# Re-emitting a long-convolution stage as a software pipeline over 128-channel units, with both forward transforms in shared matmuls

## The chip, the cores and the metric

The kernel runs on one core of one Trainium2 chip. Times are device microseconds (us) of one execution. The profile gives, for one execution, the busy time of each engine (PE is TensorE, PEld its weight loads, DVE is VectorE, ACT is ScalarE, SP is SyncE; a "q" behind a name, as in SPq, is the part of the engine that issues DMAs), what each instruction waited for, and the clock that TensorE was granted.

## The reference, cut to what matters

```python
# x, v, k: (1, 2048, 1024) bf16;  ssm_k: (1024, 2048)
a  = s5_ssm(x)                       # linear recurrence over time, complex state of 1024
kv = shift_conv(k, shift_k) * v      # 4-tap causal filter per channel, times v
y  = irfft(rfft(pad(kv)) * rfft(pad(ssm_k)))[:2048] + kv * ssm_D   # convolution of length 4096
b  = x * y
g  = sigmoid((x * gate_w).sum(-1))
out = g * a + (1 - g) * b
```

The change touches only `y`, which is called the convolution below. The convolution of 1024 channels is done with transforms written as matmuls.

## The kernel before

The program has four stretches: tables (to 35 us), the convolution, a change-over in which tables and scaled C matrices for the recurrence are made, and the scan part. The convolution works on four units of 256 channels. `front` makes the first stage of both forward transforms (`zk` from the filter, `zv` from `kv`), and each of 8 rounds does the second stages, the complex product, and the first inverse stage. `evict` means here the copy from PSUM (the matmul accumulator) to SBUF.

```python
def front(u):
    ka = load_K(u); zk = ...; stage1(ka, zk, 0)        # 8 x (4 matmuls, one eviction)
    for j in range(CH // 128):
        make_kv(u * (CH // 128) + j)                   # 4-tap filter; 3 tmpj multiplies on ScalarE; kv_scr <- acc
    va = load_A(kv_scr, u, "va")                       # same buffer as ka, bufs=1
    zv = ...; stage1(va, zv, 1)
    zs[u] = (zk, zv)

front(0)
for u in range(NU):                                    # NU = 4, CH = 256
    for kk in range(16 // KM):                         # 8 rounds
        ks = spectrum(zk, kk, fC, fS, fN, "ks")        # 6 matmuls, eviction on ScalarE
        vs = spectrum(zv, kk, fC, fS, fN, "vs")        # 6 matmuls, eviction on ScalarE
        ...                                            # t1, t2, pp: five products on VectorE
        qq = spectrum(None, kk, gC, gN, gS, "qq", inp=pp)   # 6 matmuls, eviction on ScalarE
        for i in range(KM):                            # 2 stores of 128 KB, one on SyncE, one on ScalarE
            (nc.sync if k2 % 2 == 0 else nc.scalar).dma_start(out=zb[k2:128:16, ...], in_=qq[:, i, ...])
    if u + 1 < NU: front(u + 1)
    for gg in ...:                                     # last stage: 4 matmuls, cv eviction on ScalarE, store
        nc.sync.dma_start(out=pB_scr..., in_=cv)
```

## Time and profile before

| | before |
|---|---|
| time | 761.41 us (761.37 to 761.45, 2 runs) |
| span of the profiled run | 758.3 us |
| last `cv` eviction (end of the convolution) | 426.6 us |
| from there to the end | 331.8 us |
| TensorE's granted clock, mean | 0.797 |

The page of the profile, kernel before: busy time by engine, then the span in 40 slices of 19 us (each digit is the busy share, or the clock, in tenths).

```profile
PE 449.9 (59%) x2013; PEld 218.6 (29%) x2048; DVE 431.5 (57%) x1022; ACT 368.7 (49%) x455; POOL 4.1 (1%) x10
...
PE   0030555438466546557564250679996997799567
...
DVE  6444657532323132222322513799999999998962
ACT  4765969437334543436333779722631552155022
...
PEclk9985667677767876767776665698998999899869
```

No engine stays full before slice 27. From there VectorE is at 9: the scan part is VectorE's. In the convolution (slices 3 to 23) ScalarE reaches 9 in two slices at the start, and then nothing stays above 6 for long, which is the mark of engines that wait for each other.

The groups table, kernel before: line, engine, operation, tiles, count | busy us, mean ns of one | idle time of the engine before them, and what ended it.

```profile
L333 PE MATMUL ps<-pp,gC 128*128 128x512 bf16 x64 | 36.4, 569 | 114.1 <-DVE pp L375 114.1
L318 PE MATMUL ps<-tab_188,ka 128*128 128x256 bf16 x256 | 44.5, 351 | 97.9 <-DMA ka<-kv_scr 52.0
L340 ACT CAST qq<-ps 128x1024 bf16<-128x1024 f32 x32 | 32.3, 1011 | 102.6 <-PE ps L338 102.6
```

TensorE waited 114.1 us for the product `pp`, and 52.0 us for `kv` to come back from memory. The timeline of one round shows the first wait:

```profile
207.11 0.42 DVE L375 TENSOR_TENSOR pp<-t_1036 128x512 bf16<-128x512 bf16 x1
207.59 0.61 PE L333 MATMUL ps<-pp,gC 128*128 128x512 bf16 x1 [3.43 <-DVE pp L375]
...
209.51 1.01 ACT L340 CAST qq<-ps 128x1024 bf16<-128x1024 f32 x1 [4.05 <-PE ps L338]
...
211.26 1.01 ACT L340 CAST ks<-ps 128x1024 bf16<-128x1024 f32 x1 [0.73 <-PE ps L338]
...
212.93 1.01 ACT L340 CAST vs<-ps 128x1024 bf16<-128x1024 f32 x1 [0.66 <-PE ps L338]
213.97 0.69 DVE L371 TENSOR_TENSOR t_1072<-ks,vs 128x1024 bf16<-128x1024 bf16 x1 [6.44 <-ACT vs L340]
```

The round is a loop: product, inverse matmuls, the forward matmuls of the next round, which stand behind the inverse ones in TensorE's queue, the `vs` eviction, and the product again. The longest wait of TensorE in it is 3.43 us, of ScalarE 4.05, of VectorE 6.44. The table of windows (busy us of each engine with its count, then the clock, the share of the DMA engines, GB/s) gives the sum for the convolution:

```profile
core 0: us, PE busy (x) PEld busy (x) DVE busy (x) ACT busy (x) POOL busy (x), PEclk, DMA share, GB/s
40.00:426.00 386.00, 202.89 (x884) 112.45 (x896) 137.15 (x237) 197.43 (x180) 0.00 (x0) 0.72 0.36 82
```

### The profile page before, as it was taken

To read this page: it belongs to the slowest core of one execution; us is meant where nothing else is said; L and a number is where in the kernel's file an instruction comes from. 1 tells how busy PE (TensorE), PEld (TensorE's weight loads), DVE (VectorE), ACT (ScalarE), POOL (GpSimd) and SP (SyncE) were. 2 spreads that over 40 slices of the span, in tenths; PEclk is the share of its full clock that TensorE was granted. 3 is DMA by queue.
4 is the path that set the end of the run, shared out by engine and by line. 5 is a ranking of instruction groups with operands and counts; after the bars stand their busy time and mean duration, and the time that the engine had idled before them with its cause. 6 is when DMAs were issued, how large, how long until landed. Compare 5 with 4: busy or idle time off the path is not lost.

```text
span 758.3 us, 6271 instructions
## 1 busy us (share of the span) xinstructions
PE 449.9 (59%) x2013; PEld 218.6 (29%) x2048; DVE 431.5 (57%) x1022; ACT 368.7 (49%) x455; POOL 4.1 (1%) x10
## 2 busy tenths in 40 slices
PE   0030555438466546557564250679996997799567
PEld 0020322224233323234232010334442443344223
DVE  6444657532323132222322513799999999998962
ACT  4765969437334543436333779722631552155022
POOL 2000000000000000000000000000000000000000
PEclk9985667677767876767776665698998999899869
DMA  9768974234111431132111777310312130011001
GB/s 168 127 104 187 197 160 111 85 82 118 35 28 41 108 87 29 41 70 62 35 29 40 146 142 169 113 35 22 112 55 57 57 111 15 0 57 42 0 14 43
DMA packets 124537, 59.42 MB, mean 78 GB/s; under 512 B 92632, under 2 KB 117208, under 8 KB 124504
## 3 DMA queue, kind: packets, MB, share of 16 engines
q1 hardware_dynamic: 110208, 46.15, 26.9%
q10 hardware_dynamic: 14296, 12.87, 6.9%
q8 instruction: 16, 0.26, 0.1%
q14 instruction: 17, 0.14, 0.1%
HBM read 17.06 MB, written 12.58 MB: 39 GB/s over the span
## 4 chain that ended last, share of the span: by engine, by line
DVE 37%; PE 27%; ACT 16%; DMA 8%; issue 5%; SPq 2%; ACTq 1%; DVEq 0%
PE ps L333 7%; DVE Wim L534 4%; DVE Wre L532 4%; PE ps L318 4%; DMA ka<-kv_scr 4%; PE ps L337 4%; ACT vs L340 3%; PE ps L338 3%; ACT tmpj L303 3%; DMA kv_scr<-acc 2%; PE psy L563 2%; PE psy L566 2%; DVE pp L375 1%; DVE pre_re L508 1%; PE bu_re L494 1%
## 5 line engine op out<-in xcount | busy, mean ns | idle before, releaser
L333 PE MATMUL ps<-pp,gC 128*128 128x512 bf16 x64 | 36.4, 569 | 114.1 <-DVE pp L375 114.1
L318 PE MATMUL ps<-tab_188,ka 128*128 128x256 bf16 x256 | 44.5, 351 | 97.9 <-DMA ka<-kv_scr 52.0
L340 ACT CAST qq<-ps 128x1024 bf16<-128x1024 f32 x32 | 32.3, 1011 | 102.6 <-PE ps L338 102.6
L318 PEld LDWEIGHTS <-ka 128*128 128x128 bf16 x256 | 32.1, 127 | 110.1 <-DMA ka<-kv_scr 53.2
L303 ACT ACTIVATE tmpj<-kT,skc 128x2047 bf16<-128x2047 bf16 (+2 forms) x24 | 46.8, 2002 | 22.3 <-DVE acc L305 12.1
L563 PEld LDWEIGHTS <-hb_re 128*128 128x128 bf16 x256 | 25.5, 102 | 74.2 <-DVE hb_re L543 44.5
L333 PEld LDWEIGHTS <-gC 128*128 128x128 bf16 x64 | 7.7, 120 | 126.3 <-DVE pp L375 124.7
L340 ACT CAST ks<-ps 128x1024 bf16<-128x1024 f32 x32 | 32.4, 1012 | 19.7 <-PE ps L338 19.7
L572 ACT ACTIVATE m_t<-dsk,gcols 128x512 bf16<-128x512 bf16 x32 | 22.9, 719 | 35.6 <-DVE u_t L576 35.5
L570 ACT ACTIVATE ga<-psy,gcols 128x512 bf16<-128x512 f32 x32 | 21.2, 675 | 37.9 <-PE psy L566 34.7
L501 ACT ACTIVATE bure<-bu_re 128x512 bf16<-128x512 f32 x32 | 19.0, 595 | 40.4 <-PE bu_re L494 17.1
L340 ACT CAST vs<-ps 128x1024 bf16<-128x1024 f32 x32 | 32.5, 1016 | 8.1 <-PE ps L338 8.0
L566 PEld LDWEIGHTS <-hb_im 128*128 128x128 bf16 x256 | 25.9, 102 | 36.5 <-issue 6.9
L325 ACT CAST zv<-ps 128x1024 bf16<-128x1024 f32 x24 | 22.8, 1020 | 25.7 <-PE ps L318 25.7
L305 DVE TENSOR_TENSOR acc<-acc,tmpj 128x2047 bf16<-128x2047 bf16 (+2 forms) x24 | 29.4, 1225 | 9.6 <-ACT tmpj L303 8.5
L482 PE MATMUL psg<-gwb,xT_b 128*128 128x1 bf16 x128 | 7.0, 168 | 45.0 <-ACT omg L485 26.7
L333 PE MATMUL ps<-zv,fC 128*128 128x512 bf16 x64 | 32.9, 513 | 0.6 <-ACT zv L325 0.6
L333 PE MATMUL ps<-zk,fC 128*128 128x512 bf16 x52 | 31.4, 603 | 0.0
L532 DVE TENSOR_TENSOR_SCAN Wre<-rv,init_re,pre_re 128x512 bf16<-128x512 f32 x24 | 30.7, 1278 | 0.0
L534 DVE TENSOR_TENSOR_SCAN Wim<-rv,init_im,pre_im 128x512 bf16<-128x512 f32 x24 | 30.6, 1273 | 0.0
L502 ACT ACTIVATE buim<-bu_im 128x512 bf16<-128x512 f32 x32 | 19.1, 598 | 22.3 <-PE bu_im L497 22.3
L323 DVE CAST zv<-ps 128x1024 bf16<-128x1024 f32 x8 | 9.7, 1222 | 30.6 <-PE ps L318 30.6
(796 smaller groups left out, 1251.6 us busy)
## 6 DMA issues: line engine op xcount, KB each, us to landing
kv_scr<-acc ACTq DMA_DIRECT2D x8, 512.0 KB
zb<-qq ACTq DMA_DIRECT2D x32, 128.0 KB
zb<-qq SPq DMA_DIRECT2D x32, 128.0 KB
pB_scr<-cv SPq DMA_DIRECT2D x16, 256.0 KB
out_dram<-ot SPq DMA_DIRECT2D x16, 256.0 KB
x_tt<-in_A_x_dram SPq DMA_DIRECT2D x8, 256.0 KB
pbb<-pB_scr SPq DMA_DIRECT2D x8, 256.0 KB
x_tt<-in_A_x_dram ACTq DMA_DIRECT2D x8, 256.0 KB
```

What stands on the lines that cost most here:

```text
L303: nc.scalar.activation(out=tmpj[:, j:S], in_=kT[:, 0:S - j], func=ACT.Identity, scale=col(skc, j))
L305: nc.vector.tensor_tensor(out=acc[:, j:S], in0=acc[:, j:S], in1=tmpj[:, j:S], op=ALU.add)
L318: nc.tensor.matmul(ps[:, i, :], lhsT=a[:, 4 * q + i, :], rhs=tab1.rearrange("p k r c -> p (k r c)"), start=True, stop=True)
L325: nc.scalar.copy(o, i_)
L333: nc.tensor.matmul(ps[:, i, :, :], lhsT=tC[:, k2, :], rhs=zz, start=True, stop=False)
L337: nc.tensor.matmul(ps[:, i, 0, :], lhsT=tS[:, k2, :], rhs=zz[:, 1, :], start=False, stop=(CH == 512))
L340: nc.scalar.copy(w, ps)
L532: nc.vector.tensor_tensor_scan(out=Wre, data0=rcol_bc, data1=pre_re, initial=init_re, op0=ALU.mult, op1=ALU.add)
L534: nc.vector.tensor_tensor_scan(out=Wim, data0=rcol_bc, data1=pre_im, initial=init_im, op0=ALU.mult, op1=ALU.add)
L563: nc.tensor.matmul(psy, lhsT=hb_re[:, pi, tl * 128:(tl + 1) * 128], rhs=CTr[pi][:, d0:d0 + DHW], start=(cnt == 0), stop=(cnt == n_mm - 1))
L566: nc.tensor.matmul(psy, lhsT=hb_im[:, pi, tl * 128:(tl + 1) * 128], rhs=CTi[pi][:, d0:d0 + DHW], start=(cnt == 0), stop=(cnt == n_mm - 1))
L572: nc.scalar.activation(out=m_t, in_=dsk[:, d0:d0 + DHW], func=ACT.Identity, scale=gcols[:, tt_:tt_ + 1])
```

## The change

Its intent is to break that loop. Units have 128 channels (8 of them); the two forward transforms lie in one tile `zkv`, so that one matmul with 512 columns serves both; the inverse of a round is emitted one round later (`pend`); the first stage of the next unit, the filter for the unit after that and the last stage of the unit before are dealt out between the rounds; more of the evictions go to VectorE (36 of 176; 20 before); the `tmpj` multiplies go to VectorE; every `zb` store (now 128 of 64 KB) and every other DMA of the steady loop is issued by SyncE.

```diff
-    CH = 256
+    CH = 128
@@ the filter
-                    nc.scalar.activation(out=tmpj[:, j:S], in_=kT[:, 0:S - j], func=ACT.Identity, scale=col(skc, j))
+                    nc.vector.tensor_scalar(out=tmpj[:, 0:S - j], in0=kT[:, 0:S - j], scalar1=skc[:, job, j:j + 1], ...)
-                nc.scalar.dma_start(out=kv_scr[c0:c0 + 128, :], in_=acc)
+                nc.sync.dma_start(out=kv_scr[c0:c0 + 128, :], in_=acc)
@@ second forward stage: k and kv in one matmul
+                    nc.tensor.matmul(ps[:, i], lhsT=fC[:, k2, :], rhs=z[:, k2], start=True, stop=False)
@@ inverse
+                qq = bW.tile([128, 4, 2, CH], BF16, name="qq")          # bW has bufs=2
+                evac(eng, qq, ps)
+                for i in range(4):
+                    nc.sync.dma_start(out=zb[k2:128:16]..., in_=qq[:, i]...)
@@ the loop
+            for u in range(NU):
+                ...
+                for q in range(4):
+                    spec(z, kv, q, 0, "A")
+                    stage1(a, zs[u + 1], w, 2 * (q % 2), "V")           # if u + 1 < NU
+                    spec(z, kv, q, 1, "A")
+                    pp_new = product(kv)
+                    stage1(a, zs[u + 1], w, 2 * (q % 2) + 1, "A")       # if u + 1 < NU
+                    next(kvg, None)                                     # a step of the filter, unit u + 2
+                    if pend is not None: inverse(*pend, "A")
+                    pend = (pp_new, zb, q)
+                    if zb_prev is not None and q >= 2:
+                        final(zb_prev, u - 1, q - 2, "V" if q == 2 else "A")
+                drain(kvg)
+                if u + 2 < NU: va[u + 2] = load_A(kv_scr, u + 2, "va")
+                zb_prev = zb
```

## The prediction

> **What bounds the kernel now.** The table of windows splits the 758.3 us span into table setup (to 35 us), the convolution (to about 426), a change-over in which ScalarE scales the C matrices (to 480), and the scan part (VectorE busy 35 to 40 of every 40 us). The change touches only the convolution. There no engine is full: in the steady spectrum stretches the windows show, per 20 us, PE 10 to 13.5, VectorE 4 to 6, ScalarE 7 to 8. The timeline shows a serial loop: `ks` eviction, `vs` eviction (1.02 us each), five product instructions (2.0 us together), six inverse matmuls, `qq` eviction. PE waits over 3 us for `pp` in each of 32 rounds (114 us, the groups table); a round takes about 7.8 us. Between units PE waits for `ka<-kv_scr` (52 us in all). A 256-channel unit takes 84 us (chain of waits: 157, 241, 325).
>
> **Removed, added, moved.** Work hardly changes; its order does. 176 evictions of 1024 columns before and after. Matmul columns are equal; inverse matmuls double to 384 at half the width. The 24 `tmpj` multiplies leave ScalarE (2.0 us each) for VectorE, at about 0.75 us as the same-shape `acc` tensor_scalar. The `zb` stores become 128 of 64 KB, all issued by SyncE at 0.6 us.
>
> **One 128-channel unit (an estimate from those durations):**
> - VectorE: 5 evictions x 1.15 + 4 products x 2.03 + shift 7.2 + 0.3 = 21 to 22 us
> - ScalarE: 17 evictions x 0.95 = 16 to 17 us
> - PE at full clock: 32 x 0.108 + spectrum 6.9 + inverse 4.3 + final 1.7 = 16.5 us; twice that at half clock
> - SyncE issue: 16 x 0.6 + transposes 5 + others 3 = 17 to 18 us
> - DMA: transposes 6, two loads 4.8, `zb` 5, others 5 = about 21 us.
>
> The limit is VectorE, with DMA near it. In-order queues of five nearly full engines cost some of it: I expect 25 to 27 us a unit against 42 per 128 channels now; the last unit, without stage 1 and shift, 16.
>
> PE gaps of over 3 us disappear, so its clock should rise. The Trainium skill, "TensorE: Matmul & The Clock Gate", Part 1, says that about 3.4 us of idling halves the clock. The trace agrees: 0.71 in the spectrum stretches, 0.50 after the load waits, 0.91 to 1.00 in the dense scan part.
>
> **Sum.** First spectrum at about 63 us (now 86), then 7 x 26 + 16, and 8 for the last inverse, final and store: the convolution ends near 268 instead of 426. Almost all of this is on the critical path; the 334 us after it stay. Predicted 603 us, 8 in 10 between 565 and 652. Chances: faster by over 2% 0.97, within 0.02, slower 0.01.
>
> **What would show it.** Right: convolution end between 230 and 310; PE's wait for `pp` far below 114 us; clock above 0.85 in the convolution; VectorE at 75% or more there, the others 55 to 80%; no 7 us wait for `kv_scr` after the first unit; the stretch from the last `cv` to the end within 10 us of 334. Wrong: long PE waits for an eviction or `pp`; SyncE full or stuck.
>
> **What would make it wrong.** (a) The framework's scheduler may pull all shift work forward again (all eight jobs by 145 us here) and starve the first units. (b) `zb` stores write 8 partitions; the skill's "DMA: Bandwidth & Descriptors", section on why a DMA increments its semaphore by 16, implies 8 of 16 engines; those would carry about 26 us a unit. No view separates the engines. (c) Four PSUM buffers shared by VectorE and ScalarE evictions may couple them: 33 us a unit would give about 652. (d) Faster: smaller tiles may let the change-over start earlier.

## More of the kernel before

The kernel before ran beside every experiment, with medians from 760.69 to 761.41 us, so runs of different chips and hours can be compared.

## The result

The kernel after took 644.46 us (643.72 to 645.19, 2 runs), the one before 761.41 us. The ratio is 0.8464, 95% interval 0.8422 to 0.8505. A ratio is the mean time of one kernel's runs over that of the other's of the same rounds, so it is not quite the ratio of the medians quoted.

So it is faster, and inside the range of the prediction, but 41 us above its point (603 us). The page of the profile, kernel after (slices of 16 us):

```profile
PE 410.0 (64%) x2240; PEld 212.4 (33%) x2240; DVE 465.4 (72%) x1059; ACT 306.4 (48%) x415; POOL 4.1 (1%) x10
...
PE   0023877484747493953451087999699978998577
...
DVE  7649997393939462630372389999999899989952
ACT  3832865454454664741369961264126611552042
...
PEclk9999997778887888876875578999889998999579
```

Slices 5 and 6 show what the pipeline can do: TensorE 8 and 7, VectorE 9 and 9. From slice 8 on there is a sawtooth, 3 9 3 9 3 9 on VectorE. The groups table, kernel after, says what TensorE and ScalarE wait for:

```profile
L285 ACT CAST kv<-ps 128x1024 bf16<-128x1024 f32 x64 | 64.3, 1015 | 65.8 <-PE ps L338 58.3
...
L327 PE MATMUL ps<-tab_188,va 128*128 128x256 bf16 x128 | 25.4, 341 | 57.5 <-DMA va<-kv_scr 55.7
...
L285 ACT CAST qq<-ps 128x1024 bf16<-128x1024 f32 x32 | 32.5, 1019 | 32.1 <-DMA zb<-qq 29.6
...
L356 PE MATMUL ps<-pp,gC 128*128 128x256 bf16 x128 | 32.5, 288 | 8.6 <-ACT kv L285 5.0
...
L374 PE MATMUL ps<-zb,tabFc 128*128 128x512 bf16 x32 | 15.1, 473 | 28.7 <-DMA zb<-qq 28.7
```

The wait of the inverse matmuls, 114.1 us before (all for `pp`), is down to 8.6: the loop is broken. In its place stand three waits for DMAs: for `va` (55.7 us), and for the `zb` stores by the last stage (28.7) and by the next `qq` eviction (29.6), which needs a free `qq` buffer. The windows of the whole convolution and of one unit (from one `va` load to the next), kernel after:

```profile
core 0: us, PE busy (x) PEld busy (x) DVE busy (x) ACT busy (x) POOL busy (x), PEclk, DMA share, GB/s
40.00:303.00 263.00, 159.67 (x1088) 105.70 (x1088) 169.64 (x268) 134.79 (x140) 0.00 (x0) 0.84 0.58 122
121.13:154.37 33.24, 20.94 (x136) 13.85 (x136) 21.70 (x34) 16.53 (x17) 0.00 (x0) 0.79 0.60 127
```

The busy times of a unit are those of the prediction (VectorE 21 to 22, ScalarE 16 to 17), but the unit takes 33.24 us, not 25 to 27. The DMA share of 0.60 excludes a lack of mean bandwidth as the cause. The last `cv` eviction ends at 303.8 us (268 was predicted); from there to the end are 339.6 us (334 was predicted). About 36 of the 41 us are therefore in the convolution.

The timeline of one unit, kernel after (start us, us, engine, line, operation, tiles): SyncE's DMA issues, one eviction of ScalarE, and the wait of TensorE at the end:

```profile
106.20 0.57 SPq L309 DMA_DIRECT2D kv_scr<-acc  x1
...
116.91 1.03 ACT L285 CAST qq<-ps 128x1024 bf16<-128x1024 f32 x1
...
117.97 2.54 SPq L363 DMA_DIRECT2D zb<-qq  x4
120.56 0.45 SPq L378 DMA_DIRECT2D pB_scr<-cv  x1
121.13 0.51 SPq L316 DMA_DIRECT2D va<-kv_scr  x1
...
126.16 1.03 PE L327 MATMUL ps<-tab_188,va 128*128 128x256 bf16 x4 [8.05 <-DMA va<-kv_scr]
```

`kv` of this unit was sent to memory at 106.20. The `va` load that reads it back was issued at 121.13. In between SyncE stood at a `zb` store whose `qq` was evicted at 116.91 (the ScalarE line in the fence), though TensorE had finished the matmuls for it at 107.5. The table of waits of SyncE's issuing part, kernel after, sums this up:

```profile
engine line waited for: us in total, times, longest us
SPq L363 <- ACT qq L285: 95.5, 17, 11.1
```

The Trainium skill, "DMA: Bandwidth & Descriptors", section "Anatomy of one DMA — SWDGE (gpsimd) path", says that the DMA engines do not wait on semaphores and that the issuing sequencer waits before it dispatches. The section is about DMAs issued by GpSimd; this trace shows it for SyncE: the store waits there, up to 11.1 us, and the load behind it waits with it.

Why was the `qq` eviction late? The order of the instructions as built shows it. ScalarE's evictions of a steady unit, in the order in which they stand in its queue (k is a spectrum eviction to `kv`, z a first-stage eviction to `zkv`, Q an inverse eviction to `qq`, c the last-stage eviction to `cv`):

```
as the source is written     kkzQ kkzQ kkzQ kkzQ c
as built, 2 qq buffers       kkz kkz Q k QQ k z Q kkz c
```

The framework that builds the program puts instructions into each engine's queue in an order of its own. In the kernel after, the `qq` evictions stand up to two rounds behind their matmuls and come in a bunch. With four `qq` buffers, and nothing else changed, the built order is that of the source.

### The profile page after: what moved, and what is told of

The parts are those of the page before. It is cut to its first block, busy times and chain, and to the rows that moved or that the text cites. A ratio compares the mean times of both kernels' runs of the same rounds, so it can differ in the third digit from the quotient of the medians.

```text
span 643.4 us, 6726 instructions
## 1 busy us (share of the span) xinstructions
PE 410.0 (64%) x2240; PEld 212.4 (33%) x2240; DVE 465.4 (72%) x1059; ACT 306.4 (48%) x415; POOL 4.1 (1%) x10
## 4 chain that ended last, share of the span: by engine, by line
DVE 41%; PE 21%; ACT 11%; DMA 9%; SPq 9%; issue 5%; ACTq 0%; DVEq 0%
DVE Wim L575 5%; DVE Wre L573 5%; DMA va<-kv_scr 4%; SPq L363 4%; PE ps L336 3%; ACT kv L285 3%; PE ps L327 3%; DVE acc L306 2%; PE psy L607 2%; PE psy L604 2%; PE ps L356 2%; SPq L491 2%; DVE pre_re L549 2%; DVE pre_im L555 2%; DVE hb_re L584 1%
## 5 line engine op out<-in xcount | busy, mean ns | idle before, releaser
L285 ACT CAST kv<-ps 128x1024 bf16<-128x1024 f32 x64 | 64.3, 1015 | 65.8 <-PE ps L338 58.3
L283 DVE CAST zkv<-ps 128x1024 bf16<-128x1024 f32 x28 | 34.2, 1220 | 50.0 <-PE ps L327 49.8
L327 PE MATMUL ps<-tab_188,va 128*128 128x256 bf16 x128 | 25.4, 341 | 57.5 <-DMA va<-kv_scr 55.7
L336 PE MATMUL ps<-zkv,fC 128*128 128x512 bf16 x128 | 54.7, 428 | 6.2 <-ACT kv L285 4.9
L285 ACT CAST qq<-ps 128x1024 bf16<-128x1024 f32 x32 | 32.5, 1019 | 32.1 <-DMA zb<-qq 29.6
L327 PE MATMUL ps<-tab_188,ka 128*128 128x256 bf16 x128 | 20.9, 295 | 42.0 <-DVE ka L321 41.4
L285 ACT CAST zkv<-ps 128x1024 bf16<-128x1024 f32 x36 | 36.1, 1022 | 22.1 <-PE ps L327 22.0
L607 PEld LDWEIGHTS <-hb_im 128*128 128x128 bf16 x256 | 26.1, 103 | 47.6 <-issue 18.4
L337 PE MATMUL ps<-zkv,fS 128*128 128x256 bf16 x128 | 38.4, 300 | 0.0
L338 PE MATMUL ps<-zkv,fN 128*128 128x256 bf16 x128 | 38.3, 299 | 0.0
L356 PE MATMUL ps<-pp,gC 128*128 128x256 bf16 x128 | 32.5, 288 | 8.6 <-ACT kv L285 5.0
L374 PE MATMUL ps<-zb,tabFc 128*128 128x512 bf16 x32 | 15.1, 473 | 28.7 <-DMA zb<-qq 28.7
L357 PE MATMUL ps<-pp,gN 128*128 128x128 bf16 x128 | 29.2, 228 | 0.0
```

The source lines that it names most:

```text
L283: nc.vector.tensor_copy(o, i_)
L285: nc.scalar.copy(o, i_)
L327: nc.tensor.matmul(ps[:, i, :], lhsT=a[:, 4 * q + i, :], rhs=t1v, start=True, stop=True)
L336: nc.tensor.matmul(ps[:, i], lhsT=fC[:, k2, :], rhs=z[:, k2], start=True, stop=False)
L337: nc.tensor.matmul(ps[:, i, :, 0, :], lhsT=fS[:, k2, :], rhs=z[:, k2, :, 1, :], start=False, stop=False)
L338: nc.tensor.matmul(ps[:, i, :, 1, :], lhsT=fN[:, k2, :], rhs=z[:, k2, :, 0, :], start=False, stop=True)
```

## The experiments

**Theory.** The late order of the `qq` evictions costs the missing time: a late `qq` makes its `zb` store late, SyncE stands at that store, and `va`, `zb` and the free `qq` buffer all come late. **Rivals.** (1) The place of the `va` load on SyncE is at fault, and moving the load mends it. (2) SyncE simply issues too much. (3) The `zb` stores write 8 partitions each, and if only half of the DMA engines carry them, these set the 33 us (point b of the prediction). (4) The four PSUM buffers couple the engines (point c). Correctness held in every run.

### Four `qq` buffers

```diff
-                qq = bW.tile([128, 4, 2, CH], BF16, name="qq")
+                qq = bW.tile([128, 4, 2, CH], BF16, name="qq", bufs=4)
```

> Only edit: four buffers for qq instead of two. Theory 1 (order): with two qq buffers the framework's scheduler places the qq evictions up to two rounds late on ScalarE, so the zb stores and everything behind them on SyncE's one queue (the va load) come late, and PE waits 8 to 13 us a unit for va. Then four buffers bring back the program's order, the distance between va loads falls from 33.3 us to 24 to 27 us, PE's wait for va from 56 us to under 15 us, time 600 to 615 us. Theory 2 (the zb stores of 8 partitions fill half of the DMA engines, which set the 33 us): unit time and total stay within 5 us of 644. Theory 3 (four PSUM buffers couple VectorE and ScalarE evictions): also little change, under 10 us, since the PSUM buffers stay four.

Measured: 576.57 us (one run), 68 us less than after, and better than the 600 to 615 us expected. TensorE's wait for `va` is 19.9 us, 12.7 of them once at the start; under 15 was expected. The last `cv` eviction ends at 246.8 us. The table of windows of this kernel, convolution and one unit, with the same columns as above, and SyncE's wait:

```profile
40.00:250.00 210.00, 145.70 (x1095) 100.32 (x1095) 174.74 (x281) 133.58 (x144) 0.00 (x0) 0.91 0.75 155
110.67:135.75 25.08, 18.94 (x150) 13.32 (x149) 22.07 (x35) 16.78 (x19) 0.00 (x0) 0.86 0.86 168
```

```profile
SPq L363 <- ACT qq L285: 25.8, 17, 3.2
```

The unit takes 25.08 us with the same stores, the same PSUM buffers and the same load on SyncE. That refutes rivals 2, 3 and 4 as causes of the 33 us. VectorE is busy 22.07 of 25.08 us, 88%, the limit that the prediction named; but the DMA engines' share is 0.86, and TensorE still stands for 4.4 to 6.0 us a unit before the last stage, which reads `zb`; so what sets the 25 us is not shown. But two things were changed by the edit: the number of buffers, and with it the order.

### The `va` load earlier on SyncE, and from another queue

```diff
+                    if q == 3 and u + 2 < NU: va[u + 2] = load_A(kv_scr, u + 2, "va")   # e_va_early: right after the kv_scr store
-                if u + 2 < NU: va[u + 2] = load_A(kv_scr, u + 2, "va")
```

> Only edit: the va load is emitted right after the kv_scr store of its unit, ahead of that quarter's zb stores; the build shows that it then stands behind one zb store instead of four on SyncE. Theory 1: the one zb store still waits for the late qq eviction, so only about 2.5 us a unit are won: 628 to 638 us. Theories 2 and 3: no change, 640 to 648 us.

```diff
-                nc.sync.dma_start(out=t, in_=src[...])
+                (nc.gpsimd if name == "va" else nc.sync).dma_start(out=t, in_=src[...])     # e_va_pool
```

> Only edit: the va load is issued from GpSimd's idle queue instead of SyncE's; the qq buffers stay two. Theory 1: va no longer queues behind zb stores, PE's wait for va goes from 56 us to under 15 us; the late qq evictions stay, so a unit takes 26 to 30 us, total 610 to 630 us. Theory 2 (DMA engines full): the va data would still come late, total 640 or more.

Measured: 637.55 us, as expected, and 634.49 us, a miss (one run each; four runs of one kernel, at the end, spread over 4.9 us, so gains of 7 and 10 us are small). With the load on GpSimd's queue TensorE's wait for `va` is gone but for one at the start (14.8 us), and yet only 10 us are won. The table of waits of this kernel shows where they went:

```profile
PE ps L374 <- DMA zb<-qq: 50.3, 7, 10.3
ACT qq L285 <- DMA zb<-qq: 38.2, 10, 8.2
...
PE ps L327 <- DMA va<-kv_scr: 14.8, 1, 14.8
```

The last stage now waits 50.3 us for `zb`, 28.7 in the kernel after, and the `qq` evictions 38.2 instead of 29.6; SyncE still waits 95.4 us for `qq`. (The built order of the `qq` evictions shifted a little in both runs and stayed late.) Rival 1 falls: the wait for `va` was the one that ended last, but the late `qq` evictions hold the unit by another path when it is removed.

### Every second `zb` store on ScalarE's queue

```diff
-                    nc.sync.dma_start(out=zb[k2:128:16]..., in_=qq[:, i]...)
+                    (nc.sync if k2 % 2 == 0 else nc.scalar).dma_start(out=zb[k2:128:16]..., in_=qq[:, i]...)
```

> Only edit: every second zb store is issued from ScalarE's queue, as the kernel before had it. If SyncE's issue time (0.6 us each, 16 a unit) is what counts, 8 x 0.6 = 5 us a unit come off: about 605 to 615 us. Theory 1: the order of qq evictions stays late, so va stays late; gain 0 to 15 us (629 to 644), as ScalarE also pays 5 us a unit for issuing.

Measured: 606.87 us (one run), 38 us less than after, more than the theory expected and what rival 2 expected. The run decides nothing, because the built order of ScalarE's evictions became that of the source as well. It stays above the two-buffer kernel with that order and all stores on SyncE (next): its convolution ends at 278.2 us, 30 us later than there. Why is not shown. The stores now stand in ScalarE's own queue, between its evictions, but SyncE's order changed as well; 16 loads of `xT_b`, for example, stand in the middle of the convolution.

### The order alone

Two buffers as in the change, but each ScalarE eviction of the convolution is tied behind the one emitted before it, by an edge that only orders and waits for nothing:

```diff
+                elif last_act:
+                    with tc.issue_after(last_act[-1].ins):
+                        last_act.append(nc.scalar.copy(o, i_))
```

> Two qq buffers as in the changed kernel, but ScalarE's evictions are held in the program's order by no-sync edges (the build shows the same ScalarE, PE and SyncE order in the convolution as with four buffers). It separates the order from the number of buffers, which e_qq4 (577 us) changed together. Theory 1a (the late order is the cost): about e_qq4, 575 to 595 us. Theory 1b (two buffers are too few, because an eviction must wait for the four stores of the one two rounds earlier, whatever the order): 625 to 650 us.

Measured: 589.53 us (one run), as the theory expected. In the traces the steady units of this kernel and of the kernel after have the same order of work on SyncE and VectorE and of stages on TensorE; only ScalarE's order differs. One steady unit of this kernel (columns as above), and the waits of SyncE for `qq` and of TensorE for `va`:

```profile
112.18:137.36 25.18, 17.54 (x135) 12.40 (x136) 21.81 (x34) 15.98 (x18) 0.00 (x0) 0.93 0.86 167
```

```profile
SPq L368 <- ACT qq L288: 37.2, 22, 9.8
PE ps L332 <- DMA va<-kv_scr: 13.5, 1, 13.5
```

The order alone, with two buffers, is worth 55 us: a unit takes 25.18 us instead of 33.24, SyncE's wait falls from 95.5 to 37.2 us, and TensorE waits for `va` only at the start. The convolution ends at 248.5 us, with four buffers at 246.8. So in the convolution the additional buffers buy next to nothing but the order. Of the 13 us to the kernel with four buffers, 11 lie behind the convolution.

### The late order with four buffers

Four buffers, with the evictions and stores of the inverses held back and tied so that the built order of a steady unit is that of the kernel after. The `va` load goes ahead of the held-back stores in it.

```diff
+                held.append((ps, zb, q, eng))          # in inverse(): eviction and stores come at release()
+                    if u >= 2 and q == 2: release(2)   # and at other fixed places of the loop
```

> The other half of the square: four qq buffers, but ScalarE's evictions held by no-sync edges in the late order of the changed kernel (the build shows the same string of evictions in units 2 to 6). SyncE's order is not quite that of the changed kernel: va comes before the late zb stores. Theory 1a: near the changed kernel, 620 to 645 us. Theory 1b: near e_qq4, 575 to 600 us.

Measured: 603.35 us (one run), between what the two forms of the theory expected; convolution end 273.6 us. The four runs make a square, of times in us:

| | late order | order of the source |
|---|---|---|
| 2 buffers | 644.5 (after) | 589.5 |
| 4 buffers | 603.4 | 576.6 |

The late order costs 55 us (644.5 less 589.5) with two buffers. With four the run above it takes 27 us more (603.4 less 576.6), but not for ScalarE's order alone: its trace shows that SyncE's order (the `va` load ahead of the held-back stores) and VectorE's (filter steps, and the addition to `ka`) changed with the edit, too. So neither the 27 us nor the 28 us between the two costs can be put down to one thing: the shortage of buffers, the place of the `va` load and the order of VectorE are not told apart.

### Three buffers

```diff
+                qq = bW.tile([128, 4, 2, CH], BF16, name="qq", bufs=3)
```

> Three qq buffers. The order of ScalarE's evictions as built is between the late one and the program order (two of the four qq evictions of a unit come in their place, two a round late). Theory (the order and what it delays costs the time, in steps): between the two, 590 to 630 us, with waits of the first-stage matmuls for va of a few us a unit. If two buffers were just under a threshold and any third buffer removes the stall: 577 to 585 us.

Measured: 579.07 us (one run). The built order is between the two, and not all the way back:

```
as built, 3 qq buffers       kkz kkz Q k Q k z Q kkz Q c
```

The expectation of the theory, a cost in steps (590 to 630 us), is a miss. One additional buffer with a mildly late order is 2.5 us above the single run with four and within the range of the four timed runs below (575.44 to 580.35). So half of the late evictions, with a third buffer, cost nothing that can be told from noise. That would fit a threshold, but the order and the number of buffers changed together, so of which of the two is not shown. SyncE's wait for `qq` is 35.8 us here, longest 5.1, against 95.5 and 11.1 in the kernel after.

### The 11 us behind the convolution

The kernel after waits once more at the end of the convolution. VectorE's table generator writes `ht`, and the table of waits has `DVE ht L473 <- DMA pB_scr<-cv: 14.0, 1, 14.0`. I read this as a reuse of memory: `ht` lies where `cv` lay, so it waits for the last `cv` store, and SyncE issues that behind 12 transposing loads of `xT_b`, which take it 15.48 us. In the kernels with four `qq` buffers, everything that is placed after `qq` lies 4 KB further on, and `ht` starts before the last `cv` eviction. First the store was moved:

```diff
-                nc.sync.dma_start(out=pB_v[...], in_=cv)
+                (nc.scalar if u == NU - 1 else nc.sync).dma_start(out=pB_v[...], in_=cv)
```

> The changed kernel with one edit: the last unit's two cv stores are issued from ScalarE's queue. In the changed kernel they stand behind twelve xT transposes on SyncE (issued at 311.6 us, the evictions ended at 303.8), and the first ht of the change-over waits 14 us for them. If that wait sets the start of the scan part: 10 to 14 us less, 630 to 635 us. If the change-over is bound by ScalarE's 32 scalings of 1.04 us and by the C transposes behind the same xT transposes: 0 to 4 us less, 640 to 645 us.

Measured: 643.80 us (one run), no gain. On ScalarE's queue the second store was issued only at 309.58 us, and `ht` began at 314.1, against 316.2; the timeline puts its wait down to a load of `xT_b` now. That leaves the theory neither shown nor refuted, so the placement was tested by itself: the kernel with the forced order and two buffers, plus 4 KB a partition that nothing reads.

```diff
+                if not padded:
+                    padded.append(bW.tile([128, 4, 2, CH], BF16, name="qpad"))     # 2 buffers of 2 KB
+                    nc.gpsimd.memset(padded[0][:, 0, 0, 0:2], 0.0)
```

> Program order forced and two qq buffers, as g_order2 (589.5 us), plus 4 KB a partition of padding that nothing reads, so that everything allocated after it lies where it lies with four buffers. If the rest of the difference to e_qq4 (13 us, all of it after the last cv eviction) is the placement of the table generator's tile ht, which then need not wait for cv's last store: 576 to 582 us, and ht starts before the last cv eviction. If it is instead the two further qq buffers themselves (the last units' stores finishing earlier): 587 to 592 us, and ht starts 11 to 13 us after it.

Measured: 578.92 us (one run), as expected if it is the placement. The timelines of VectorE, first without the padding, then with it:

```profile
245.75 1.22 DVE L285 CAST cv<-ps 128x1024 bf16<-128x1024 f32 x1 [9.18 <-PE ps L380]
261.59 0.88 DVE L478 TENSOR_SCALAR ht<-iota_row,thn 128x512 f32<-128x512 f32 x2 [14.62 <-DMA pB_scr<-cv]
```

```profile
244.38 0.88 DVE L482 TENSOR_SCALAR ht<-iota_row,thn 128x512 f32<-128x512 f32 x2 [7.56 <-DMA xT_b<-in_A_x_dram]
...
247.06 1.22 DVE L286 CAST cv<-ps 128x1024 bf16<-128x1024 f32 x1
```

The last `cv` stores are issued no earlier with the padding (at 259.49 us; without it at 256.98), and `ht` no longer cares. The convolution ends at the same time (249.2 and 248.5 us), and the rest takes 327.9 us instead of 339.2. So the placement in memory, which changes no data dependence, held the change-over. That the tile in the way is `cv` is my reading of the wait; addresses are not in the trace. It fits that in the kernel with the stores on two queues, which has two buffers and no padding but issues its last `cv` stores at once (276.72 us), `ht` waits 7.1 us and the rest takes 326.9 us.

### A further step: half of the C scalings on VectorE

With four buffers, VectorE waits 28.9 us in the change-over for ScalarE to scale the C matrices (`DVE CrT L502 <- ACT c_t L501`). So two of every four scalings go to VectorE:

```diff
-                nc.scalar.activation(out=t2, in_=cim, func=ACT.Identity, scale=col(mc2i, pi))
+                nc.vector.tensor_scalar(out=t2, in0=cim, scalar1=col(mc2i, pi), scalar2=None, op0=ALU.mult)
```

(and the same for `t4`).

> e_qq4 plus one edit in the change-over: 16 of the 32 scalings of the C matrices go from ScalarE (1.04 us each) to VectorE as bf16 tensor_scalar (about 0.45 us each). In e_qq4 ScalarE is busy 52 of the 60 us from 240 to 300. If ScalarE bounds the change-over: 12 to 17 us less than e_qq4, 560 to 565 us. If SyncE's transposes bound it (the last C transpose lands at about 281 us, the scan starts at 299): 5 to 10 us less, 567 to 572 us.

Measured: 566.51 us (one run), 10 us less; between the two branches that were expected. Finally both better kernels were timed, with repetitions:

> The change with four qq buffers, timed: 576 to 578 us, ratio to the kernel before 0.756 to 0.760.

> Four qq buffers and half of the C scalings on VectorE, timed: 566 to 568 us, ratio to the kernel before 0.742 to 0.747.

| kernel | median us (range of 4 runs) | ratio to before, 95% interval |
|---|---|---|
| change + 4 `qq` buffers | 578.06 (575.44 to 580.35) | 0.7589 (0.7563 to 0.7616) |
| the same + half of the C scalings on VectorE | 565.21 (564.4 to 565.91) | 0.7422 (0.7407 to 0.7437) |

The first time is within 0.1 us of its expected range and its ratio is inside it; the second time is 0.8 us below its range, and its ratio is inside. Both beat the change itself. VectorE's wait for ScalarE at the C matrices no longer shows; what VectorE waits for in its place is the transposing load of C (10.6 us, 8 times).

## Why the prediction was right and where it was off

- **The verdict and the range** held: 644.46 us lies between 565 and 652, and faster by over 2% was given 0.97. The point, 603, was 41 us too low. That the range held is partly luck: its upper end stands for 33 us a unit by the coupling of PSUM buffers, point (c); a unit did take 33.24 us, but from a cause that the prediction did not name.
- **"A serial loop" bounds the kernel before:** right, though the `qq` eviction, which it counts in, ran beside the next forward matmuls. The wait before the inverse matmuls, 114.1 us for `pp`, became 8.6 (3.6 of them for `pp`) when the inverse was moved by a round.
- **The sums of one unit** were right: VectorE 21 to 22 predicted, 21.70 measured; ScalarE 16 to 17, 16.53 measured. The `tmpj` multiply took 0.751 us on VectorE, 0.75 predicted. The Trainium skill, "VectorE: DVE Perf Modes", section "The perf-mode tier table", gives 693 ns for such a multiply of 2048 bf16 elements and 1224 ns for a product of two tensors; the trace has 746 and 1224 ns, so it agrees on the second and is 8% above on the first. TensorE's 16.5 us was given for full clock; it measured 20.94 at a clock of 0.79, and 18.94 at 0.86.
- **First spectrum at 63 us:** right, 62.9 (its first matmul).
- **"I expect 25 to 27 us a unit":** this is the step that failed. The mechanism was allowed for ("In-order queues of five nearly full engines cost some of it"), but the term was mis-sized: 33.24 us measured. The sum took the program order of the source as the order in the queues. With two `qq` buffers the built order puts the inverse evictions up to two rounds late, SyncE stands at their stores (95.5 us), and `va`, `zb` and `qq` come late. With the order restored, and only that, the convolution ends at 248.5 us; with four buffers a unit takes 25.08 us.
- **"No 7 us wait for `kv_scr` after the first unit":** wrong for this reason: of the 55.7 us in 6 waits, 13.1 are the first, and the other five took 8.1 to 9.9 each. The sign named for the wrong case, "SyncE full or stuck", is what showed: stuck, not full.
- **Convolution end near 268 (230 to 310 allowed):** 303.8. The kernel with the order restored ends 20 us before 268, so the estimate was cautious for a pipeline that runs as written: there the units 0, 5 and 6 took 16.7, 18.4 and 18.7 us (from first `kv` eviction to first `kv` eviction) where the sum has 26 for each.
- **VectorE at 75% or more there:** wrong, 169.64 of 263 us, 64%, for the same reason; 174.74 of 210, 83%, with four buffers. ScalarE, at 134.79 us or 51%, was also below its 55 to 80%.
- **Clock above 0.85:** a near miss, 0.84. The Trainium skill, "TensorE: Matmul & The Clock Gate", Part 1, ties the clock to idle stretches of about 3.4 us; the trace agrees in direction: the clock of the convolution was 0.72 before, with 37 idle stretches of TensorE over 3 us (172 us together), 0.84 after, with 10 (79 us), and 0.91 with four buffers, with 6 (43 us). The clock is not the cause of the long unit: TensorE is busy 2.00 us less in the unit of 25.08 us, which is 8.16 us shorter.
- **Rest within 10 us of 334:** right, 339.6, but by the placement of `ht` it holds about 11 us that need not be there.
- **What could make it wrong:** (a) did not happen, in that the units started on time. (b), the 8 partitions of a `zb` store, is refuted as the cause of 33 us (its 26 us were an estimate): the same stores fit into 25.08 us, at a mean DMA share of 0.86. Whether they would stop a still shorter unit is open. (c) is refuted likewise. (d) happened in the variants, by placement: `ht` starts ahead of the last `cv` eviction.

What stays open is why the building step chose the late order; only that it depends on the number of `qq` buffers is shown (two, three and four give three orders). Also open are how the 28 us by which the late order costs more with two buffers than with four divide, and what sets the 25 us of a unit with the order restored.

## What to carry to other kernels

A software pipeline written in the source is only a wish: read the order in which the evictions and DMA issues stand in each engine's queue before you sum up engine times, and give the tile that a store reads enough buffers: here their number changed the order. On an in-order DMA issuer one store that waits for a late producer delays every load behind it; here, taking the load off that queue gained 10 us, removing the lateness 55. When a stage boundary waits for a store that nothing needs, look for a tile that reuses its memory.

## What the Trainium skill lacked or had wrong

- "DMA: Bandwidth & Descriptors", section "Issuing engines are not separate DMA queues", says that issuing from several engines saves only the sequencer's time to initiate, "which is usually small relative to the DMA itself". Here a 64 KB store took SyncE 0.597 us (median of 128), 16 of them 9.6 us of a unit of 25 to 33 us, and a transposing load 1.3 to 4.3 us. The DMAs' own time was not read beside it, so the sentence is not refuted, but these issue times were not small against the unit. The page also does not say that a waiting store holds back the loads behind it on the same issuer: 95.5 us in the kernel after.
- No page that was used here says that the framework which builds the program can order an engine's instructions otherwise than the source, depending on a tile's buffer count: 644.5, 579.1 and 576.6 us with two, three and four `qq` buffers.
- No page that was used here warns that where a tile lies can make a later stage wait for a store of an earlier one: 4 KB of unused padding took 589.5 us to 578.9 us.
- "VectorE: DVE Perf Modes", section "The perf-mode tier table", gives 693 ns for `tensor_scalar` on 2048 bf16 elements; the trace has 746 ns (median of 8).
